# Gated linear attention into a gated SSM: q, k and alpha loaded as 32-step squares and turned by VectorE, output stores on the ACT queue

## The chip, the cores and the metric

The kernel runs on one core of a Trainium2 chip. The metric is the device time of one execution in microseconds. An execution that was also profiled gives the span and the trace that this document reads.

## The reference

Four sequences of 768 steps, 8 heads, 48 channels per head. First a recurrence per head with a gate per channel, then a block with an input projection, a scan over time, a gate and an output projection:

```
state = alpha[:, :, t, :, None] * state + einsum('bhd,bhe->bhde', k[:, :, t], v[:, :, t])
y[:, :, t] = einsum('bhd,bhde->bhe', q[:, :, t], state)
x = y as (B, S, H*D)                                # 4, 768, 384
val, gate = split(x @ w_in)                         # 384 x 1024, handed over as float64
h = exp(A_log)[0] * h + val[:, t]                   # scan over t
out = (gate * sigmoid(gate) * h) @ w_out            # 512 x 384
```

## The kernel before, in words

**Tiling.** A group is 256 steps (two tiles of 128) of one sequence with all heads, so there are N = 12 groups, three to a sequence. A pair j of heads shares the 128 partitions of a transposed tile: head 2j in rows 0 to 47, head 2j+1 in rows 64 to 111, with padding rows between (`DP` = 64). 

**Stages of one group.** `load` (L205) brings alpha, q and k into padded tiles `pads[n % 2]` (two sets) and v into one of three `v_sb`, by `load_heads` (L78): two DMAs of 128 partitions x 8 heads x 48 floats for each input, eight in all, on SP's queue. `front(n)` (L278) has five steps: (1) TensorE transposes alpha (L295, eight 128x128 tiles, in two PSUM tiles `tp`), VectorE makes the running products V from the group's end backward (L302), their reciprocal start iV and the running products P forward (L307), and ScalarE makes two passes over V into a tile `junk` that nobody reads, for their accumulated outputs (L312, L314), which test the range of V; (2) q is transposed and multiplied by P into Q (L319); (3) k is transposed and multiplied by V into K (L323); (4) scores `sc` = K against Q in 64-step blocks (L332), masked into A (L335); (5) K is turned back into Kn (L119, L120). `back(n)` (L341) makes block states `z` (L131), their running sums S_n on VectorE (L357), the outputs `y` inside a block (L146), a small ScalarE read `fence` (L151), then those from earlier blocks (L164), copies to x_sb (L365, L367), and transposes to xT (L173, L174). `ssm(n)` (L85) has four projections `pj` of twelve matmuls (L93), here called pj0 to pj3, each followed by the scan hh on VectorE (L96), Silu into sg on ScalarE (L101) and their product f on VectorE (L102); and two output tiles `o` of eight matmuls (L107), each copied to o_sb by ScalarE (L110) and stored (L111). The tiles pj and o share two PSUM buffers in turn.

**Order.** It is written out by hand (`manual_schedule`, L415 to L451). A turn n of the loop interleaves front(n), back(n-1), the first four steps of ssm(n-2) and the last two of ssm(n-3). TensorE's order in a full turn is: transposes of alpha(n), z(n-1), o(n-3) twice, transposes of q(n), y inside, pj0(n-2), transposes of k(n), y before, pj1, sc(n), tpx (x_sb), pj2, tpk (K back), pj3. VectorE's: V, P, S_n, Q, hh0, f0, K, hh1, f1, A, hh2, f2, hh3, f3. ScalarE's: junk twice, o_sb twice, fence, sg0, x_sb, sg1, xT, sg2, Kn, sg3. In turn n, `load(n + 2)` is called after the third step of front(n); on SP's queue it stands behind the stores of the same turn. Every queue works in its order.

**Weights.** w_in and w_out come as float64 words in twelve units (`fetch_unit`, L223); units 0 to 5 are fetched at the start, 6 to 11 in turn 0, behind the loads of group 2 on SP's queue. `split_unit` and `join_unit` turn a unit into float32 with ScalarE, VectorE and GpSimd, one unit to a step of turns 0 to 2, each of them in line with the other work of its engine.

**DMA semaphores.** DMAs raise eight completion semaphores (DMAHW0 to DMAHW7), handed out in turn in the order of the built program's text. Before a DMA is issued, its queue waits until the DMA that last had the same semaphore has landed, eight DMAs back in that text.

Of the kernel before, what the change touches and what calls it, by code (L numbers as in the profile page):

```python
# [9 lines left out]
FP32 = mybir.dt.float32  # L10
U8 = mybir.dt.uint8
# [7 lines left out]
def kernel(  # L19
# [23 lines left out]
    nc = tc.nc  # L43
    B, H, S, D = q.shape
    DM = H * D
    DI = moe_A_log.shape[0]
    C = 128
    R = 64
    NR = C // R
    G = 2  # L50
    GC = G * C
    GR = G * NR
    NG = S // GC
    NP = H // 2
    DP = 64
# [22 lines left out]
    def load_heads(dst, src, n, queue=nc.sync):  # L78

        b, g = divmod(n, NG)  # L80
        for c in range(G):
            rows = ds(g * GC + c * C, C)
            queue.dma_start(out=dst[:, c, :, 0:D], in_=src[b, :, rows, :].rearrange("h p d -> p h d"))  # L83

    def ssm(n, xT, prev_h, pool, ps_mm):  # L85

        b, g = divmod(n, NG)
        f = pool.tile([C, NI, GC], FP32, name="f")
        for cc in range(NI):
            pj = ps_mm.tile([C, 2, GC], FP32, tag="mm", name="pj")  # L90
            for i in range(2):
                for kk in range(NK):
                    nc.tensor.matmul(pj[:, i, :], w_in[:, kk, i, ds(cc * C, C)], xT[:, kk, :],  # L93
                                     start=(kk == 0), stop=(kk == NK - 1))
            hh = pool.tile([C, GC], FP32, tag=f"h{cc}", name="hh")
            nc.vector.tensor_tensor_scan(  # L96
                out=hh, data0=a_dec[:, cc:cc + 1].to_broadcast([C, GC]), data1=pj[:, 0, :],
                initial=prev_h[cc][:, GC - 1:GC] if g else 0.0, op0=ALU.mult, op1=ALU.add)
            prev_h[cc] = hh
            sg = pool.tile([C, GC], FP32, name="sg")  # L100
            nc.scalar.activation(sg, pj[:, 1, :], AF.Silu)  # L101
            nc.vector.tensor_mul(f[:, cc, :], sg, hh)  # L102
            yield
        for c in range(G):
            o = ps_mm.tile([C, DM], FP32, tag="mm", name="o")
            for cc in range(NI):
                nc.tensor.matmul(o, f[:, cc, ds(c * C, C)], w_out[:, cc, :],  # L107
                                 start=(cc == 0), stop=(cc == NI - 1))
            o_sb = pool.tile([C, DM], FP32, name="o_sb")
            nc.scalar.activation(o_sb, o, AF.Copy)  # L110
            nc.sync.dma_start(out=out[b, ds(g * GC + c * C, C), :], in_=o_sb)  # L111
            yield

    def keys_back(K, Kn, ps_tp):
# [66 lines left out]
    def ranged(ctx):  # L181
# [4 lines left out]
        p1 = pool("p1", 1)  # L186
# [15 lines left out]

        vs, st, xs = {}, {}, {}

        def load(n, names="aqkv", queue=nc.sync):  # L205
            for name in names:
                if name == "v":
                    vs[n] = p3.tile([C, G, H, D], FP32, name="v_sb")
                dst = vs[n] if name == "v" else pads[n % NBUF][name]
                load_heads(dst, dict(a=alpha, q=q, k=k, v=v)[name], n, queue)  # L210

# [64 lines left out]
        def front(n):  # L278

            pad = pads[n % NBUF]  # L280
            V = Vs[n % 2]
            iV0 = p2.tile([C, NP], FP32, name="iV0")
            P = p1.tile([C, NP, GC], FP32, name="P")
            Q = p3.tile([C, NP, GC], FP32, name="Q")
            K = p2.tile([C, NP, GC], FP32, name="K")
            A = As[n % 2]
            Kn = p2.tile([C, G, NP, C], FP32, name="Kn")
            st[n] = dict(V=V, Q=Q, A=A, Kn=Kn)

            def turned(name, jj):  # L290
                tp = ps_tp.tile([C, 2, GC], FP32, tag="tp", name="tp")
                for u in range(2):
                    j = 2 * jj + u
                    for c in range(G):
                        nc.tensor.transpose(tp[:, u, ds(c * C, C)], pad[name][:, c, 2 * j:2 * j + 2, :], ident)  # L295
                return tp

            for jj in range(NP // 2):
                tp = turned("a", jj)
                js = slice(2 * jj, 2 * jj + 2)  # L300
                for u in range(2):
                    nc.vector.tensor_tensor_scan(out=V[:, 2 * jj + u, GC - 1::-1], data0=tp[:, u, ::-1],  # L302
                                                 data1=bias[:, 1:2].to_broadcast([C, GC]), initial=1.0,
                                                 op0=ALU.mult, op1=ALU.max)
                nc.vector.reciprocal(iV0[:, js], V[:, js, 0])
                for u in range(2):
                    nc.vector.tensor_tensor_scan(out=P[:, 2 * jj + u, :], data0=tp[:, u, :],  # L307
                                                 data1=bias[:, 1:2].to_broadcast([C, GC]),
                                                 initial=iV0[:, 2 * jj + u:2 * jj + u + 1],
                                                 op0=ALU.mult, op1=ALU.max)  # L310
            junk = p1.tile([C, NP, GC], FP32, name="junk")
            nc.scalar.activation(junk, V[:, :, 0:GC], AF.Relu, scale=-1.0 / LOW, bias=bias[:, 0:1],  # L312
                                 accum_out=left[:, n, 0:1])
            nc.scalar.activation(junk, V[:, :, 0:GC], AF.Relu, scale=1.0 / HIGH, bias=bias[:, 2:3],  # L314
                                 accum_out=left[:, n, 1:2])
            yield
            for jj in range(NP // 2):
                js = slice(2 * jj, 2 * jj + 2)
                nc.vector.tensor_mul(Q[:, js], turned("q", jj), P[:, js])  # L319
            yield  # L320
            for jj in range(NP // 2):
                js = slice(2 * jj, 2 * jj + 2)
                nc.vector.tensor_mul(K[:, js], turned("k", jj), V[:, js, 1:GC + 1])  # L323
            yield
            sc = ps_sc.tile([C, 2, 512], FP32, tag="sc", name="sc")
            scv = sc.rearrange("p i (x t) -> p i x t", t=R)
            for c in range(G):
                for j in range(NP):
                    for r in range(NR):
                        for i in range(2):  # L330
                            rows, steps = ds(DP * i, DP), ds(c * C + R * r, R)
                            nc.tensor.matmul(scv[ds(R * r, R), i, c * NP + j, :], K[rows, j, steps],  # L332
                                             Q[rows, j, steps], start=True, stop=True, skip_group_check=True)
            for i in range(2):
                nc.vector.copy_predicated(out=A[:, i].rearrange("p x t -> p (x t)"),  # L335
                                          mask=mask[:, ds(i * GP * R, GP * R)], data=sc[:, i])
            yield
            keys_back(K, Kn, ps_tp)
            yield

        def back(n):  # L341

            s = st.pop(n)
            v_sb = vs.pop(n)
            first, last = n % NG == 0, n % NG == NG - 1
            S_n = p2.tile([C, GR, NP, D], FP32, name="S_n")
            if not first:
                nc.gpsimd.tensor_mul(S_n[:, 0], S_end[0], s["V"][:, :, 0:1].to_broadcast([C, NP, D]))  # L348
            zv = block_states(s["Kn"], v_sb, ps_sc, "sc")
            S_end[0] = None if last else p2.tile([C, NP, D], FP32, name="S_end")  # L350
            for x in range(GR):
                src = zv[:, x % NR, x // NR]
                dst = S_n[:, x + 1] if x + 1 < GR else S_end[0]
                if first and x == 0:
                    nc.vector.tensor_copy(out=dst, in_=src)
                elif dst is not None:
                    nc.vector.tensor_add(dst, S_n[:, x], src)  # L357
            yield
            yv = values_inside(s["A"], v_sb, ps_y, p2, 1)
            yield  # L360
            values_before(yv, s["Q"], S_n, first, 1)
            x_sb = p2.tile([C, G, DM], FP32, name="x_sb")
            xv = x_sb.rearrange("p g (j i e) -> p i (g j) e", i=2, e=D)
            ys = yv.rearrange("p i g j e -> p i (g j) e")
            nc.scalar.activation(xv[:, 0], ys[:, 0], AF.Copy)  # L365
            for r in range(NR):
                nc.scalar.activation(xv[ds(R * r, R), 1], ys[ds(R * (1 - r), R), 1], AF.Copy)  # L367
            yield
            xs[n] = p2.tile([C, NK, GC], FP32, name="xT")
            features(x_sb, xs[n], ps_tp)  # L370
            yield
# [247 lines left out]
```

## Time and profile before

| | us |
|---|---|
| median of 3 runs | 353.29 (352.75 to 353.89) |
| the profiled execution | 352.41 |
| its span | 350.7 |
| TensorE busy | 311.7 (89%) |
| VectorE busy | 201.1 (57%) |
| ScalarE busy | 113.4 (32%) |
| GpSimd busy | 57.9 (17%) |

The span is the profiled part of an execution; 1.7 us lie around it. "Busy" is the time in which an engine has an instruction under way. Rows of groups give the engine, the operation, the shapes and the mean duration of one. In a timeline, each line has a start, a length, an engine and a source line; what stands in brackets is idle time before it and what ended that. The chain of waits follows the work that ended last back to its start, at each step to what released it. SPq and ACTq are the queues of SyncE and ScalarE that issue DMAs.

### The profile page before, as it was taken

To read this page: it belongs to the slowest core of one execution; us is meant where nothing else is said; L and a number is where in the kernel's file an instruction comes from. 1 tells how busy PE (TensorE), PEld (TensorE's weight loads), DVE (VectorE), ACT (ScalarE), POOL (GpSimd) and SP (SyncE) were. 2 spreads that over 40 slices of the span, in tenths; PEclk is the share of its full clock that TensorE was granted. 3 is DMA by queue.
4 is the path that set the end of the run, shared out by engine and by line. 5 is a ranking of instruction groups with operands and counts; after the bars stand their busy time and mean duration, and the time that the engine had idled before them with its cause. 6 is when DMAs were issued, how large, how long until landed. Compare 5 with 4: busy or idle time off the path is not lost.

```text
span 350.7 us, 9637 instructions
## 1 busy us (share of the span) xinstructions
PE 311.7 (89%) x4233; PEld 251.7 (72%) x4233; DVE 201.1 (57%) x373; ACT 113.4 (32%) x243; POOL 57.9 (17%) x77
## 2 busy tenths in 40 slices
PE   2445763899999999999999999999999999998994
PEld 1334652687887887887878878868878878776682
DVE  2939968567449448546566476384494485313140
ACT  1514564332324233313314324333342233222111
POOL 4388898640000000000000000000000000000000
PEclk9996585999999999999999999999999999999999
DMA  9999995440850921902904905908301010010101
GB/s 128 216 228 192 288 190 71 79 57 2 150 79 2 186 42 48 170 13 64 163 3 99 129 2 116 113 2 165 64 12 36 2 47 2 2 48 0 49 0 53
DMA packets 107650, 29.02 MB, mean 83 GB/s; under 512 B 100944, under 2 KB 107088, under 8 KB 107600
## 3 DMA queue, kind: packets, MB, share of 16 engines
q1 hardware_dynamic: 104992, 27.93, 45.1%
q10 hardware_dynamic: 2608, 0.40, 1.0%
q8 instruction: 35, 0.57, 0.7%
q14 instruction: 15, 0.12, 0.1%
HBM read 23.60 MB, written 4.72 MB: 81 GB/s over the span
## 4 chain that ended last, share of the span: by engine, by line
PE 80%; POOL 5%; SPq 5%; DVE 3%; DMA 3%; issue 3%; ACT 0%; POOLq 0%; DVEq 0%; ACTq 0%
PE pj L93 36%; PE o L107 18%; PE tp L295 7%; SPq L83 4%; PE z L131 4%; PE y L164 3%; PE sc L332 3%; PE y L146 3%; DMA bits<-in_moe_w_in_dram 3%; PE tpk L119 2%; PE tpx L173 2%; POOL ex L241 2%; SPq L227 1%; POOL w_in L251 1%; POOL w_in L250 1%
## 5 line engine op out<-in xcount | busy, mean ns | idle before, releaser
L93 PE MATMUL pj<-xT,w_in 128*128 128x256 f32 x576 | 134.2, 384 | 0.0
L93 PEld LDWEIGHTS pj<-xT,w_in 128*128 128x128 f32 x576 | 106.2, 190 | 14.2
L107 PE MATMUL o<-w_out,f 128*128 128x384 f32 x192 | 65.0, 492 | 0.0
L96 DVE TENSOR_TENSOR_SCAN hh<-a_dec,hh,pj 128x256 f32<-128x256 f32 x32 | 23.9, 747 | 68.5 <-PE pj L93 68.5
L101 ACT ACTIVATE sg<-pj 128x256 f32<-128x256 f32 x48 | 18.4, 384 | 119.9 <-DVE hh L96 119.9
L107 PEld LDWEIGHTS o<-w_out,f 128*128 128x128 f32 x192 | 35.5, 190 | 23.0 <-DVE f L102 0.5
L348 POOL TENSOR_TENSOR S_n<-S_end,V 128x192 f32<-128x192 f32 x8 | 4.3, 542 | 209.6 <-DVE S_end L357 209.6
L102 DVE TENSOR_TENSOR f<-sg,hh 128x256 f32<-128x256 f32 x48 | 20.9, 435 | 23.8 <-ACT sg L101 23.8
L307 DVE TENSOR_TENSOR_SCAN P<-tp,iV,bias 128x256 f32<-128x256 f32 x48 | 33.4, 738 | 0.8
L302 DVE TENSOR_TENSOR_SCAN V<-tp,bias 128x256 f32<-128x256 f32 x48 | 30.1, 670 | 5.1 <-PE tp L295 5.1
L312 ACT ACTIVATE junk<-V,bias 128x1024 f32<-128x1024 f32 x12 | 13.8, 1148 | 53.9 <-DVE V L302 53.9
L295 PE MATMUL tp<-ident,q_pad 128*128 128x128 f32 x96 | 15.4, 305 | 14.5 <-DVE P L307 7.8
L295 PE MATMUL tp<-ident,a_pad 128*128 128x128 f32 x96 | 14.6, 300 | 14.2 <-issue 6.6
L295 PEld LDWEIGHTS tp<-ident,q_pad 128*128 128x128 f32 x96 | 12.4, 157 | 18.9 <-issue 16.3
L96 DVE TENSOR_TENSOR_SCAN hh<-a_dec,pj 128x256 f32<-128x256 f32 x16 | 11.0, 685 | 25.8 <-PE pj L93 25.8
L295 PEld LDWEIGHTS tp<-ident,a_pad 128*128 128x128 f32 x96 | 12.4, 154 | 16.0 <-issue 7.0
L241 POOL TENSOR_SCALAR ex<-ex 128x384 uint32<-128x384 uint32 x12 | 18.5, 1543 | 16.6 <-DVE ex L236 16.2
L332 PEld LDWEIGHTS sc<-Q,K 64*64 64x64 f32 x768 | 14.3, 148 | 4.3 <-issue 3.0
L335 DVE COPY_PREDICATED A<-mask,sc 128x512 f32<-128x512 uint8 x24 | 16.0, 721 | 1.1 <-PE sc L332 1.1
L332 PE MATMUL sc<-Q,K 64*64 64x64 f32 x768 | 16.1, 237 | 0.5 <-DVE K L323 0.5
L146 PEld LDWEIGHTS y<-v_sb,A 64*64 64x64 f32 x768 | 13.8, 149 | 2.7 <-issue 2.7
L295 PE MATMUL tp<-ident,k_pad 128*128 128x128 f32 x96 | 14.5, 299 | 1.4 <-DVE Q L319 1.0
(60 smaller groups left out, 325.0 us busy)
## 6 DMA issues: line engine op xcount, KB each, us to landing
a_pad<-in_alpha_dram SPq DMA_DIRECT2D x24, 192.0 KB, 4.6
k_pad<-in_k_dram SPq DMA_DIRECT2D x24, 192.0 KB, 5.5
v_sb<-in_v_dram SPq DMA_DIRECT2D x24, 192.0 KB, 5.0
out_dram<-o_sb SPq DMA_DIRECT2D x24, 192.0 KB, 2.3
q_pad<-in_q_dram SPq DMA_DIRECT2D x22, 192.0 KB, 5.0
bits<-in_moe_w_in_dram SPq DMA_DIRECT2D x8, 384.0 KB, 5.1
bits<-in_moe_w_out_dram SPq DMA_DIRECT2D x4, 384.0 KB, 7.2
q_pad<-in_q_dram ACTq DMA_DIRECT2D x2, 192.0 KB, 5.5
```

What stands on the lines that cost most here:

```text
L93: nc.tensor.matmul(pj[:, i, :], w_in[:, kk, i, ds(cc * C, C)], xT[:, kk, :], start=(kk == 0), stop=(kk == NK - 1))
L96: nc.vector.tensor_tensor_scan(out=hh, data0=a_dec[:, cc:cc + 1].to_broadcast([C, GC]), data1=pj[:, 0, :], initial=prev_h[cc][:, GC - 1:GC ...
L101: nc.scalar.activation(sg, pj[:, 1, :], AF.Silu)
L102: nc.vector.tensor_mul(f[:, cc, :], sg, hh)
L107: nc.tensor.matmul(o, f[:, cc, ds(c * C, C)], w_out[:, cc, :], start=(cc == 0), stop=(cc == NI - 1))
L146: nc.tensor.matmul(yv[at, i, c, j, :], A[rows, i, c * NP + j, :], v_sb[rows, c, 2 * j + i, :], start=(c == 0 and j == 0), stop=False, skip ...
L241: nc.gpsimd.tensor_scalar(out=ex, in0=ex, scalar1=896.0, scalar2=1151.0, op0=ALU.max, op1=ALU.min)
L295: nc.tensor.transpose(tp[:, u, ds(c * C, C)], pad[name][:, c, 2 * j:2 * j + 2, :], ident)
L302: nc.vector.tensor_tensor_scan(out=V[:, 2 * jj + u, GC - 1::-1], data0=tp[:, u, ::-1], data1=bias[:, 1:2].to_broadcast([C, GC]), initial=1 ...
L307: nc.vector.tensor_tensor_scan(out=P[:, 2 * jj + u, :], data0=tp[:, u, :], data1=bias[:, 1:2].to_broadcast([C, GC]), initial=iV0[:, 2 * jj ...
L332: nc.tensor.matmul(scv[ds(R * r, R), i, c * NP + j, :], K[rows, j, steps], Q[rows, j, steps], start=True, stop=True, skip_group_check=True)
L335: nc.vector.copy_predicated(out=A[:, i].rearrange("p x t -> p (x t)"), mask=mask[:, ds(i * GP * R, GP * R)], data=sc[:, i])
```

## The change

From group 2 on (`BY_VECTOR` = 2), alpha, q and k are no longer loaded as 128-partition tiles. Each is loaded in sixteen DMAs of 32 partitions x 8 x 32 or 16 floats, which lay 32 steps by 32 channels of each head as a square, so that VectorE's 32 x 32 block transpose of the whole 128 x 1024 tile gives what TensorE's eight transposes gave. Three such instructions to a group are new (into aT, and in place into Q and K); the multiplications then read SBUF instead of PSUM. Groups 0 and 1 stay as they were. v is loaded as before. For groups 2 and 3 GpSimd sets the padding of the squares, two memsets to a tile. The store of the output is issued by ScalarE instead of SP. Q has two buffers instead of three, K and x_sb one instead of two, and `junk` is written as bytes.

```
--- before.py
+++ after.py
@@ -108,7 +108,7 @@
                                  start=(cc == 0), stop=(cc == NI - 1))
             o_sb = pool.tile([C, DM], FP32, name="o_sb")
             nc.scalar.activation(o_sb, o, AF.Copy)
-            nc.sync.dma_start(out=out[b, ds(g * GC + c * C, C), :], in_=o_sb)
+            nc.scalar.dma_start(out=out[b, ds(g * GC + c * C, C), :], in_=o_sb)
             yield
 
     def keys_back(K, Kn, ps_tp):
@@ -202,12 +202,33 @@
 
         vs, st, xs = {}, {}, {}
 
+
+
+        BY_VECTOR, W = 2, 32
+
+        def squares(n, name):
+            return pads[n % NBUF][name].rearrange("p c h d -> p (c h d)")
+
         def load(n, names="aqkv", queue=nc.sync):
+            b, g = divmod(n, NG)
             for name in names:
+                src = dict(a=alpha, q=q, k=k, v=v)[name]
                 if name == "v":
                     vs[n] = p3.tile([C, G, H, D], FP32, name="v_sb")
-                dst = vs[n] if name == "v" else pads[n % NBUF][name]
-                load_heads(dst, dict(a=alpha, q=q, k=k, v=v)[name], n, queue)
+                    load_heads(vs[n], src, n, queue)
+                elif n < BY_VECTOR:
+                    load_heads(pads[n % NBUF][name], src, n, queue)
+                else:
+                    dst = squares(n, name).rearrange("p (j w e) -> p j w e", j=NP, e=W)
+                    for j in range(NP):
+                        for i in range(2):
+                            for half in range(2):
+                                ch, rows = min(W, D - W * half), ds(DP * i + W * half, W)
+                                if n < BY_VECTOR + NBUF and j == 0 and ch < W:
+                                    nc.gpsimd.memset(dst[rows, :, :, ch:W], 1.0 if name == "a" else 0.0)
+                                queue.dma_start(out=dst[rows, j, :, 0:ch],
+                                                in_=src[b, 2 * j + i, ds(g * GC, GC), ds(W * half, ch)]
+                                                .rearrange("(w p) d -> p w d", p=W))
 
 
 
@@ -281,8 +302,8 @@
             V = Vs[n % 2]
             iV0 = p2.tile([C, NP], FP32, name="iV0")
             P = p1.tile([C, NP, GC], FP32, name="P")
-            Q = p3.tile([C, NP, GC], FP32, name="Q")
-            K = p2.tile([C, NP, GC], FP32, name="K")
+            Q = p2.tile([C, NP, GC], FP32, name="Q")
+            K = p1.tile([C, NP, GC], FP32, name="K")
             A = As[n % 2]
             Kn = p2.tile([C, G, NP, C], FP32, name="Kn")
             st[n] = dict(V=V, Q=Q, A=A, Kn=Kn)
@@ -295,9 +316,13 @@
                         nc.tensor.transpose(tp[:, u, ds(c * C, C)], pad[name][:, c, 2 * j:2 * j + 2, :], ident)
                 return tp
 
+            by_vector = n >= BY_VECTOR
+            if by_vector:
+                aT = p1.tile([C, NP, GC], FP32, name="aT")
+                nc.vector.transpose(aT.rearrange("p j t -> p (j t)"), squares(n, "a"))
             for jj in range(NP // 2):
-                tp = turned("a", jj)
                 js = slice(2 * jj, 2 * jj + 2)
+                tp = aT[:, js] if by_vector else turned("a", jj)
                 for u in range(2):
                     nc.vector.tensor_tensor_scan(out=V[:, 2 * jj + u, GC - 1::-1], data0=tp[:, u, ::-1],
                                                  data1=bias[:, 1:2].to_broadcast([C, GC]), initial=1.0,
@@ -308,19 +333,23 @@
                                                  data1=bias[:, 1:2].to_broadcast([C, GC]),
                                                  initial=iV0[:, 2 * jj + u:2 * jj + u + 1],
                                                  op0=ALU.mult, op1=ALU.max)
-            junk = p1.tile([C, NP, GC], FP32, name="junk")
+            junk = p1.tile([C, NP, GC], U8, name="junk")
             nc.scalar.activation(junk, V[:, :, 0:GC], AF.Relu, scale=-1.0 / LOW, bias=bias[:, 0:1],
                                  accum_out=left[:, n, 0:1])
             nc.scalar.activation(junk, V[:, :, 0:GC], AF.Relu, scale=1.0 / HIGH, bias=bias[:, 2:3],
                                  accum_out=left[:, n, 1:2])
             yield
+            if by_vector:
+                nc.vector.transpose(Q.rearrange("p j t -> p (j t)"), squares(n, "q"))
             for jj in range(NP // 2):
                 js = slice(2 * jj, 2 * jj + 2)
-                nc.vector.tensor_mul(Q[:, js], turned("q", jj), P[:, js])
-            yield
+                nc.vector.tensor_mul(Q[:, js], Q[:, js] if by_vector else turned("q", jj), P[:, js])
+            yield
+            if by_vector:
+                nc.vector.transpose(K.rearrange("p j t -> p (j t)"), squares(n, "k"))
             for jj in range(NP // 2):
                 js = slice(2 * jj, 2 * jj + 2)
-                nc.vector.tensor_mul(K[:, js], turned("k", jj), V[:, js, 1:GC + 1])
+                nc.vector.tensor_mul(K[:, js], K[:, js] if by_vector else turned("k", jj), V[:, js, 1:GC + 1])
             yield
             sc = ps_sc.tile([C, 2, 512], FP32, tag="sc", name="sc")
             scv = sc.rearrange("p i (x t) -> p i x t", t=R)
@@ -359,7 +388,7 @@
             yv = values_inside(s["A"], v_sb, ps_y, p2, 1)
             yield
             values_before(yv, s["Q"], S_n, first, 1)
-            x_sb = p2.tile([C, G, DM], FP32, name="x_sb")
+            x_sb = p1.tile([C, G, DM], FP32, name="x_sb")
             xv = x_sb.rearrange("p g (j i e) -> p i (g j) e", i=2, e=D)
             ys = yv.rearrange("p i g j e -> p i (g j) e")
             nc.scalar.activation(xv[:, 0], ys[:, 0], AF.Copy)
```

## Prediction

> **What bounds the kernel now.** I read the page first. TensorE is busy 89% of the span and is 80% of the chain of waits; the rest of the chain is the start.
>
> ```profile
> span 350.7 us, 9637 instructions
> PE 311.7 (89%) x4233; PEld 251.7 (72%) x4233; DVE 201.1 (57%) x373; ACT 113.4 (32%) x243; POOL 57.9 (17%) x77
> PEclk9996585999999999999999999999999999999999
> PE 80%; POOL 5%; SPq 5%; DVE 3%; DMA 3%; issue 3%; ACT 0%; POOLq 0%; DVEq 0%; ACTq 0%
> ```
>
> Then one turn in the chain of waits (start, length): it is TensorE alone.
>
> ```profile
> 203.75 0.87 PE tp L295 x8
> 204.63 1.08 PE z L131 x64
> 205.71 5.36 PE o L107 x16
> 211.06 0.87 PE tp L295 x8
> 211.94 1.08 PE y L146 x64
> 213.01 2.79 PE pj L93 x12
> 215.80 0.87 PE tp L295 x8
> ...
> 220.54 1.09 PE sc L332 x64
> ...
> 228.50 0.87 PE tp L295 x8
> ```
>
> From 203.75 to 228.50 a turn takes 24.74 us, three entries of 0.87 among it being the transposes that go. Turns 3 to 11 (79.9 to 302.6) are all like this. Last the timelines of ScalarE and of SP's queue in the same turn, and two lines of the start:
>
> ```profile
> 209.48 1.15 ACT L312 ACTIVATE junk<-V,bias 128x1024 f32<-128x1024 f32 x1 [4.47 <-DVE V L302]
> 211.90 0.85 ACT L110 ACTIVATE o_sb<-o 128x384 f32<-128x384 f32 x2
> ```
> ```profile
> 212.40 0.83 SPq L111 DMA_DIRECT2D out_dram<-o_sb  x2
> ```
> ```profile
> 40.06 0.60 DVE L236 TENSOR_SCALAR ex<-bits 128x384 uint32<-128x384 uint32 x1 [0.21 <-DMA bits<-in_moe_w_in_dram]
> ```
> ```profile
> 60.32 1.96 PE L146 MATMUL y<-v_sb,A 64*64 64x48 f32 x64
> ```
>
> The reader is to see: o_sb starts at 211.90 though o ended at 211.06, since junk stands before it and waits for V; two DMA issues start 0.83 - 0.36 (one store's issue, by the tile's row) = 0.47 us apart; the conversion of weight unit 6 already waits for its DMA; and after TensorE had idled 5.45 us the same 64 matmuls took 1.96 us instead of 1.08.
>
> **What the Trainium skill says.** "VectorE: DVE Perf Modes", The three transpose paths: VectorE turns 32x32 blocks only, SBUF to SBUF. No transpose is in this trace. "Vector Engine (DVE) Microarchitecture Reference", 3.8: one element per cycle per lane; "VectorE: DVE Perf Modes", The TRN2 errata, has fp32 tensor_tensor at (N+151)/0.96 ns: 691 for N = 512, and the trace has 682 for Q. So my estimate for 1024 is 1.22 us. "DMA: Bandwidth & Descriptors", Issuing engines are not separate DMA queues: another issuing engine saves issue time only; no run here shows it yet. "TensorE: Matmul & The Clock Gate", Part 1: an idle window of some 3.4 us halves the clock; the y line above and PEclk's 6, 5, 8 agree.
>
> **The change, part by part.**
> *Removed from TensorE:* 3 x 0.87 = 2.61 us a turn, which would make 22.13.
> *Added to VectorE:* three transposes of 1.2 each; below 1.07 (1024 elements at one a cycle) it can't be, twice it, 2.4, is the far end. VectorE is busy 14.9 of the turn's 24.74, so its sum fits; its places matter.
> *SP:* 48 + 2 issues a group instead of 8; at 0.47 that is 23.5 us. The span of one issue hardly depends on size (332 ns smallest for a store, 368 for k); I keep 0.42 and 0.6 as ends. Packets go from 8192 to 14336 a group (six times 2048 of 128 or 64 bytes, and v); at the 23 ns that a packet costs now (DMA share 0.5 x 24.74 us x 16 / 8448) it is 21 us of each DMA engine, under the turn.
> *Stores:* two issues of 0.47 now stand in ScalarE's order, behind each o_sb.
> *Semaphores:* in the built program's text the stores of turn m (from 6 on) stand amid the k squares of group m: k's sixth and ninth DMA (37 and 40 of the 50, from 0) have the semaphore of the first and second store. They wait until those stores have landed. In turn 5 it is 42 and 44; the stores of turns 3 and 4 hold up DMAs 17 and 19 of group 4, 5 and 7 of group 5, a turn before they are wanted. Before, SP went past a turn's stores with the loads of two groups on; now the k of the same turn waits for them.
> *Pools, byte junk, memsets:* K and x_sb with one buffer are freed a turn earlier by TensorE's order (tpk and tpx before the next writes): nothing. Byte junk: no row; I take 1.15 as now, half of it is the other end (1.1 us less before o_sb). Twelve memsets of 0.3 to 0.6 lie in GpSimd's wait for unit 6: nothing.
>
> **One turn, from the end of pj3 (time 0; 203.75 before).** hh3 and f3 end at 1.7 (205.47). Transpose of alpha: 2.9. First V to last V takes 4.06 (205.39 to 209.45): 7.0. Two junk take 2.45 (to 211.90): 9.5. o_sb 0.48: 10.0; store issue at 10.1; second o_sb to 11.05; second store at 11.1. A store lands 2.3 us after issue (median): 12.4 and 13.4. TensorE is at pj0 after z, o, y = 7.5, and waits for o_sb's PSUM buffer until 10.1, ends it at 12.9, y and pj1 at 16.8. VectorE: hh0 and f0 take 1.57 after pj0: 14.5, free for the transpose of k. But k's DMAs 40 to 47 go out from 13.4, the last at 13.4 + 7 x 0.47 = 16.7; landing 2.2 (3.2 is the smallest of a load now, of which 1.0 goes on draining its 1024 packets, the median length of an issue in a backlog): 18.9. Transpose 20.1, K's two halves 0.64 each: 21.4; sc, whose first part needs one half, in effect from 21.2. From sc to the end of pj3 7.95 (220.54 to 228.50): 29.2 us, 4.5 more than now. In turn 5 only four DMAs follow the store: 27.3. Turns 3 and 4 have their k; there f0's 14.5 leads to K at 17.0, sc from 16.8: 24.8, no gain, since o_sb and K take the place of TensorE. Is SP's rest in time? From 17.2 v, a, q take 34 x 0.47 = 16: alpha has landed at 27.5 (wanted at 30.9), q at 35.3 (wanted at 39). Yes.
> TensorE now idles 2.6 and 4.4 us a turn, at which the clock may drop: between 0 and 3 us a turn (y alone lost 0.9); I take 1.3 for seven turns.
>
> **The start.** Group 2's fifty issues stand before unit 6. They begin at 23.9 as now; the first eight wait for weight units in flight (the last issued by 23.8, landing 5.5 by the median: until 29.3), the other 42 x 0.47 end at about 49.2; landing 4.7 (smallest of these rows): unit 6 at 53.9 instead of 40.06, 13.8 later. VectorE, ScalarE and GpSimd stand behind it. Turn 2 adds transposes of alpha, q and k on the chain to sc(2), with less wait for TensorE: 3.2. Shift 17 (ends 11, when all issues are at 0.47 and landing is 4, and 20).
>
> **The sum.** 17 + 2 x 0.1 + 2.6 + 6 x 4.5 + 7 x 1.3 = 56. The profiled span 350.7 becomes 407, its own time 352.41 becomes 408, and the median of 353.29 becomes 409. The tail from turn 12 has no front: nothing.
>
> **Rivals.** (A, my forecast, 0.75) as above. Its own range: turn 28.2 (issue 0.42, landing short, half junk) to 33 (transposes twice, landings 3.2): 385 to 435. (B, 0.10) k is in time after all, because issue or landing is much quicker than it looks: turns of 24.8, only the start lost: 353.3 + 17 + 0.9 = 371. For it: stores land in 1.9 at best; against it: eight issues alone take 3.3 us. (C, 0.10) SP or the small packets set the turn: at 0.7 us an issue 35 us a turn, seven turns 72 more, start 27: 452. For it: issues of 1 us[...]; against it: 256 packets an issue instead of 1024. (D, 0.04) The other side: TensorE stays the bound at 22.1 a turn, because junk, transposes and k all end before 7.5, 10 and 14.2: 9 x 2.61 = 23.5 gained, 17 lost: 347. It decides when the mean turn is under 24.74 - 17/9 = 22.85; but the chain f3, transpose, V, junk, o_sb, pj0 alone is 2.6 us too long for that. That the squares are not turned by VectorE is excluded: the built program has three such instructions a group and no transposes on TensorE. The last 0.01 is no change.
>
> **Numbers.** Range: 375 to 445 leaves out D, over half of B and most of C, 0.18. Faster by over 0.3% 0.04 (D), same 0.01, slower 0.95; 0.3% is about what a measurement of this kernel can tell from none.
>
> **What would show it.** Right: turns of 29 to 31 us from z to z, sc waiting for K, K's transpose for a DMA, SPq waiting for stores amid k; unit 6's conversion waiting until about 54; transposes of 1.2 us; issues 0.47 apart; half clock after the idle. Wrong: turns of 22 (D) or 25 (B), SPq without idle time (C), transposes over 2 us.

## The result and the profile after

| | before | after |
|---|---|---|
| median | 353.05 us (352.75 to 353.89, 4 runs) | 428.96 us (427.24 to 433.85, 4 runs) |
| ratio to before | | 1.213 (95% interval 1.208 to 1.218) |
| the profiled execution, its span | 352.41, 350.7 | 433.85, 432.1 |
| z of turn 3 starts at | 80.87 | 107.27 |
| z of turn 3 to z of turn 12 (nine turns) | 221.8 | 274.8 |
| z of turn 12 to the end | 48.0 | 50.1 |

The forecast was 409 us with a range of 375 to 445; the kernel is 76 us slower. The execution that left the profile is the longest of the four (the spans of the others are 425.5 to 427.7), so some 5 of the 81.4 us that the table explains are its own.

The page of the kernel after, lines that answer to those shown of before:

```profile
span 432.1 us, 9699 instructions
PE 310.9 (72%) x3993; PEld 243.5 (56%) x3993; DVE 242.3 (56%) x403; ACT 115.3 (27%) x243; POOL 65.6 (15%) x89
PEclk9996659559989899898799698799699898699899
SPq 28%; PE 25%; DVE 18%; DMA 12%; issue 6%; POOL 5%; ACT 4%; ACTq 0%; DVEq 0%; POOLq 0%
```

TensorE has 240 instructions fewer, but is busy as long as before: the clock row shows why, with its 7s and 6s all through the span. The chain of waits was TensorE for 80%; it is now TensorE for 25%, and SP's queue for 28%.

One turn (turn 9, z at 286.53) in the chain of waits, each line a start, a length and what it is:

```profile
288.21 1.26 DVE aT L322
...
293.60 1.25 ACT junk L337 x2
...
296.12 0.38 ACT o_sb L110
...
296.52 1.87 DMA out_dram<-o_sb
298.42 0.31 SPq L229
...
302.89 0.44 SPq L229
...
303.38 2.15 DMA k_pad<-in_k_dram
...
305.56 1.25 DVE K L349
...
307.67 2.07 PE sc L361 x64
309.74 1.47 PE tpx L173 x6
311.21 3.27 PE pj L93 x12
```

Read it downward: alpha's transpose, V, junk, o_sb, the store; SP stands until the store has landed at 298.39 and goes on with k's squares; the last of them is issued at 302.89 and lands 2.15 later; then K's transpose and sc. After that sc, tpx and pj2 take 6.81 us where at full clock they take 1.09 + 0.81 + 2.59 = 4.49.

The views of waits of the same kernel (engine, line, what it waited for: us in total, times, longest), for all engines and for SP's queue:

```profile
DVE K L349 <- DMA k_pad<-in_k_dram: 28.9, 7, 5.5
PE sc L361 <- DVE K L352: 28.4, 8, 5.4
PE pj L93 <- ACT o_sb L110: 22.2, 9, 2.5
```
```profile
SPq L229 <- DMA out_dram<-o_sb: 61.8, 9, 24.5
```

K's transpose waits for its DMA in seven turns, and SP waits for a store in nine. In each of turns 3 to 11 the load that has the semaphore of the first store is issued within 0.02 us of that store's landing. The longest of SP's waits, 24.5 us, is in turn 3, and comes back below.

### The profile page after: what moved, and what is told of

Read it like the earlier page. It is cut to its first block, busy times and chain, and to the rows that moved or that the text cites. A ratio compares the mean times of both kernels' runs of the same rounds, so it can differ in the third digit from the quotient of the medians.

```text
span 432.1 us, 9699 instructions
## 1 busy us (share of the span) xinstructions
PE 310.9 (72%) x3993; PEld 243.5 (56%) x3993; DVE 242.3 (56%) x403; ACT 115.3 (27%) x243; POOL 65.6 (15%) x89
## 4 chain that ended last, share of the span: by engine, by line
SPq 28%; PE 25%; DVE 18%; DMA 12%; issue 6%; POOL 5%; ACT 4%; ACTq 0%; DVEq 0%; POOLq 0%
SPq L229 23%; PE pj L93 15%; DVE V L327 6%; PE o L107 4%; DVE P L332 4%; DMA out_dram<-o_sb 3%; SPq L83 3%; DMA q_pad<-in_q_dram 3%; DVE aT L322 3%; DMA bits<-in_moe_w_in_dram 2%; DMA k_pad<-in_k_dram 2%; ACT junk L337 2%; PE sc L361 2%; POOL ex L262 2%; PE tpx L173 2%
## 5 line engine op out<-in xcount | busy, mean ns | idle before, releaser
L93 PE MATMUL pj<-xT,w_in 128*128 128x256 f32 x576 | 147.8, 412 | 22.2 <-ACT o_sb L110 22.2
L93 PEld LDWEIGHTS pj<-xT,w_in 128*128 128x128 f32 x576 | 115.8, 207 | 40.7 <-ACT o_sb L110 23.3
L164 PE MATMUL y<-S_n,Q 64*64 64x48 f32 x704 | 15.9, 238 | 38.7 <-ACT fence L151 38.7
L361 PE MATMUL sc<-Q,K 64*64 64x64 f32 x768 | 22.5, 290 | 28.5 <-DVE K L352 28.4
L164 PEld LDWEIGHTS y<-S_n,Q 64*64 64x64 f32 x704 | 14.4, 152 | 43.7 <-issue 27.2
L337 ACT ACTIVATE junk<-V,bias 128x1024 uint8<-128x1024 f32 x12 | 13.8, 1150 | 69.7 <-DVE V L327 69.7
L332 DVE TENSOR_TENSOR_SCAN P<-aT,iV,bias 128x256 f32<-128x256 f32 x40 | 28.6, 757 | 0.7
L349 DVE STREAM_TRANSPOSE K<-k_pad 128x1024 f32<-128x1024 f32 x10 | 12.4, 1244 | 28.9 <-DMA k_pad<-in_k_dram 28.9
L327 DVE TENSOR_TENSOR_SCAN V<-aT,bias 128x256 f32<-128x256 f32 x40 | 26.0, 693 | 0.4
L96 DVE TENSOR_TENSOR_SCAN hh<-a_dec,pj 128x256 f32<-128x256 f32 x16 | 10.9, 684 | 24.1 <-PE pj L93 24.1
L364 DVE COPY_PREDICATED A<-mask,sc 128x512 f32<-128x512 uint8 x24 | 16.1, 723 | 2.2 <-PE sc L361 1.5
L110 ACT ACTIVATE o_sb<-o 128x384 f32<-128x384 f32 x24 | 11.6, 484 | 19.9 <-PE o L107 15.7
## 6 DMA issues: line engine op xcount, KB each, us to landing
bits<-in_moe_w_in_dram SPq DMA_DIRECT2D x8, 384.0 KB, 5.5
bits<-in_moe_w_out_dram SPq DMA_DIRECT2D x4, 384.0 KB, 6.6
```

The costliest lines, as they stand in the source:

```text
L96: nc.vector.tensor_tensor_scan(out=hh, data0=a_dec[:, cc:cc + 1].to_broadcast([C, GC]), data1=pj[:, 0, :], initial=prev_h[cc][:, GC - 1:GC ...
L164: nc.tensor.matmul(yv[at, i, c, j, :], Q[rows, j, ds(R * x, R)], S_n[rows, x, j, :], start=False, stop=(c == G - 1 and j == NP - 1), skip_ ...
```

## The experiments

The theory that the forecast stood on: the semaphores that stores and k's squares share make k wait for the same turn's stores. Rivals: SP's fifty issues, or their small packets, set the turn; the stores cost only their two issues; the start is lost to something other than the order of the loads. For each run: its median, its ratio to before with the 95% interval, when z of turn 3 starts, and the mean of the nine turns from there to z of turn 12.

| | median us | ratio | z of turn 3 | mean turn |
|---|---|---|---|---|
| before | 353 | 1 | 80.87 | 24.64 |
| after | 428.96 | 1.213 (1.208 to 1.218) | 107.27 | 30.53 |
| e1, stores on SP | 395.62 | 1.117 (1.112 to 1.122) | 107.23 | 26.37 |
| e2, stores on GpSimd | 391.89 | 1.109 (1.107 to 1.112) | 108.51 | 25.73 |
| e3, before with stores on ScalarE | 353.13 | 1.000 (0.999 to 1.001) | 80.87 | 24.64 |
| e4, weight units first | 428.38 | 1.210 (1.206 to 1.214) | 92.96 | 31.95 |
| e5, 24 unread matmuls a turn | 450.20 | 1.273 (1.269 to 1.278) | 107.33 | 32.48 |
| e6, e2 and units first | 377.60 | 1.067 (1.065 to 1.070) | 91.38 | 26.11 |
| e7, e2, squares from group 4 | 366.51 | 1.037 (1.034 to 1.040) | 80.94 | 25.87 |
| e8, e2 and junk later | 385.81 | 1.091 (1.086 to 1.095) | 106.71 | 25.21 |
| e9, 12 unread matmuls a turn | 419.56 | 1.190 (1.184 to 1.195) | 106.57 | 29.12 |
| e10, q and k only, from group 4 | 341.97 | 0.968 (0.965 to 0.970) | 81.95 | 23.27 |
| e11, e6 without memsets | 382.07 | 1.080 (1.076 to 1.085) | 86.65 | 26.91 |
| e12, e2 with 5 unread matmuls | 384.03 | 1.088 (1.085 to 1.090) | 107.55 | 24.86 |

### Do the stores hold up k? (e1, e2, e3, e4)

e1: `nc.scalar.dma_start(out=out[...])` becomes `nc.sync.dma_start`. 

> The changed kernel, with the output stores back on SP's queue. Theory (the stores and the k squares of the same turn are tied through the shared DMA semaphores, so that SP stops amid k until the stores have landed): in SP's own order a store stands behind the loads of a later group, so the wait falls on a semaphore that is long free; k is in time, the turn is what 52 issues of 0.49 us on SP or the chain to o_sb allow, 25.5 to 26.5 us instead of 32; 7 turns x 6 us less: about 385 to 395 us. The stall of SP for stores (24.5 us in nine waits) is gone. Rival 1 (SP's rate of issue or the small packets set the turn): SP has two issues more per turn, so no gain, 428 to 435 us. Rival 2 (the stores on ScalarE cost only their two issues): 2 x 0.5 x 10 = 10 us less, about 418 us.

e2: the same line on `nc.gpsimd`. 

> The changed kernel, with the output stores on GpSimd's queue, whose DMAs have semaphores of their own. Theory (shared semaphores): no store stands in the order of SP's semaphores, turns of 25 to 26.5 us, 385 to 395 us, near the version with the stores on SP. Rival 1 (SP's issues or packets): 428 us. Rival 2 (a new wait: GpSimd is held at o_sb, with T and bits behind it): between 395 and 415 us.

e3: the kernel before, that line on `nc.scalar`. 

> The kernel before, with nothing changed but the output stores on ScalarE's queue. Theory: with 10 loads a group instead of 50, a load that takes a store's semaphore is wanted a turn or more later; no change, 352 to 355 us. Rival (ScalarE's issue, or its wait, costs by itself): 2 x 0.5 x 12 = up to 12 us more, 365 us.

Measured: 395.6, 391.9 and 353.1. No turn of e1 or e2 waits for a store amid k, their turns are 24.8 to 26.6 us (but for e1's turn 11, below), and 33 to 37 of the 76 us are gone by moving two DMAs a turn to another queue. In e3 the move costs nothing that can be measured (the interval ends at 0.1% more). So it is neither ScalarE's issue nor the queue as such, but which load the store's semaphore falls on. In e1, SP's order puts the stores among alpha's squares two groups on. There they have another price: in turn 11 o_sb can't be written (4.6 us of wait) because the store that has its buffer stands behind SP's loads; that turn is 32.3 us. (The "24.5 us in nine waits" of e1's expectation is the longest wait alone; the nine sum to 61.8.)

e4, in turn 0:

```
-                if n + 2 < N:
-                    load(n + 2)
                 if n == 0:
                     for u in range(6, len(units)):
                         fetch_unit(u)
+                if n + 2 < N:
+                    load(n + 2)
```

> The changed kernel, with the issues of weight units 6 to 11 moved ahead of group 2's fifty in the first turn. Theory (the loads of group 2 delay unit 6, which landed at 57.8 us instead of 40.1): unit 6 lands near 40 again, turn 3 begins up to 17 us earlier; the memsets of GpSimd, the transposes of group 2 and the longer turns stay: 408 to 413 us. Rival (the start is long because of the transposes, memsets and group 2's own late landing): no more than 5 us less, 423 to 428 us.

Measured: 428.4, no gain, and yet the rival is wrong too: z of turn 3 comes 14.3 us earlier. Turns 3 and 4 then take 33.7 and 34.0 us instead of 26.5 and 26.3, which gives it all back. My words "the longer turns stay" were the fault. In the built program's text of e4 the stores of turn 3 have the semaphores of the fourth and seventh of group 3's k, and those of turn 4 the sixth and ninth of group 4's; in the kernel after they have those of q of group 4 and alpha of group 5. The coupling to the same turn's k begins two turns sooner. The timelines of SP's queue (start, length, queue, line, DMA, count) show the first of these stands; after, then e4:

```profile
94.24 33.06 SPq L229 DMA_DIRECT2D q_pad<-in_q_dram  x16
```
```profile
77.67 34.22 SPq L229 DMA_DIRECT2D k_pad<-in_k_dram  x16
```

Sixteen issues take some 9 us elsewhere; here 24.5 and 25.8 us of waiting for the first store lie among them. In the kernel after SP was at group 4's loads while TensorE was still in turn 2, and loses 24.5 us of that lead.

### What does the clock cost? (e5, e9, e12)

e5, ten of these ahead of pj0 and fourteen ahead of sc in turns 3 to 11, into a PSUM tile that nobody reads:

```
+            for i in range(count):
+                nc.tensor.matmul(wm[:, i % 2, :], ident, w_in[:, 0, 0, 0:GC], start=True, stop=True)
```

> The changed kernel, with matmuls that nobody reads in TensorE's idle time of turns 3 to 11: ten ahead of pj0, fourteen ahead of sc. Theory (after the idle of 2.5 and 5 us TensorE works at half clock for a while, which costs about 1.6 us in turns 3 and 4 and 2 to 4 in each later one): sc, tpx and pj2 take 1.1, 0.8 and 2.6 us again, turns 3 and 4 24.8 us, later turns 29 to 30: 7 x 2.5 + 2 x 1.6 = 20 less, about 408 us. Rival 1 (the loop is held by SP, whose 50 issues take 28.5 us a group and which waits some 4 us for stores): clock at full but turns stay near 31, 425 us or more. Rival 2 (the added matmuls come out of the time of the path): slower than 429.

A miss of mine: one such matmul is two passes of 0.216 us, so that 10.4 us went into a turn, not 5.2. All turns are 32.48 us at full clock, TensorE without a gap. It shows that the idle is what halves the clock, but not what that costs.

e9: the same with 5 and 7. 

> The changed kernel again with matmuls that nobody reads, half as many: five ahead of pj0, seven ahead of sc, in turns 3 to 11 (each is two passes of 0.216 us, so the first try put 10.4 us into a turn instead of 5.2, and TensorE, 22.1 + 10.4 = 32.5, set the turn at full clock). TensorE has now 27.3 us a turn, less than the loop through the stores. Theory (the clock's loss is about 1.6 us in turns 3 and 4 and about 2.5 in the later ones, over the loop of 29.2 that the forecast worked out): turns of 29 to 30 from turn 5 on, about 409 us. Rival 1 (the loop through the stores, or SP, holds the turn at 31 to 32 whatever the clock): 425 us or more. Rival 2 (the clock still falls with so few matmuls): between the two.

Measured: 419.6, between the theory and rival 1, and not for the reason that I gave for such a value. Turns 3 to 8 are all 27.6 to 27.7 us, which is TensorE with the added matmuls; turns 9, 10 and 11 are 32.0, 34.0 and 30.1. In this program's text the stores of turns 3 to 7 fall on loads that are wanted a turn later, those of turn 8 on the twelfth of k's squares of the same group, of turn 9 on the eighth, of turns 10 and 11 on the fourth. So the added matmuls moved the semaphores as well, and the price of the clock can't be read from this run. What it does show is the coupling once more: stores on ScalarE's queue cost nothing in six turns, and 2.4 to 6.3 us in those where k of the same turn has the semaphore with eight squares or more still to come.

e12: e2, with five matmuls ahead of pj0 only. 

> The version with the stores on GpSimd's queue (391.9 us), with five matmuls that nobody reads (ten passes of 0.22 us) ahead of pj0 in turns 3 to 11, so that TensorE's idle of 2.5 us before pj0 becomes one of 0.3. No store's semaphore and no k is waited for there, so the turns differ by the clock alone: 24.8 us, and 26.3 to 26.6 where pj0 takes 4.5 us instead of 2.8. Theory (idle of 2.5 us brings the half clock after it, which costs 1.7 us in every turn that has it): all pj0 take 2.8 us, turns of 24.8 to 25.0, six turns x 1.6 = 10 less: about 382 us; SP's last load, at 312 us, comes no earlier, and if its lead is used up by then the last turns wait for k: up to 386. Rival (the half clock comes from load over a longer time, not from the idle before it): the turns stay mixed, 390 us or more.

Measured: 384.0, 7.9 less (the spans differ by 9.0), and no pj0 of turns 3 to 11 takes over 2.9 us. One of e12's turns in the view by stretches (the stretch, its length, then the busy time of TensorE, of its weight loads, of VectorE, ScalarE and GpSimd; the third number from the end is the share of the clock), and two of e2's:

```profile
132.38:157.29 24.91, 24.76 (x329) 19.25 (x329) 19.22 (x31) 8.04 (x18) 1.59 (x3) 1.00 0.47 74
```
```profile
108.51:133.33 24.82, 22.40 (x335) 17.45 (x334) 18.52 (x30) 8.08 (x18) 1.32 (x2) 1.00 0.47 75
133.33:159.90 26.57, 24.09 (x319) 18.45 (x318) 19.29 (x31) 8.06 (x18) 1.59 (x3) 0.94 0.47 73
```

TensorE's work of a turn is 22.4 us at full clock. In e2 five of the nine turns have up to 1.7 more, in pj0 after 2.5 us of idle. With the idle filled, all turns are 24.8 to 24.9.

Which of e2's turns pay can be read from its trace. The clock falls to half for 3.41 us at a time, and these stretches start (144.38, 195.58, 246.78, 274.09, 325.29) whole multiples of 3.413 us apart: 15, 15, 8 and 15. Three stretches of this grid, the first two from turn 4, the third from turn 5:

```profile
140.97:144.38 3.41, 0.98 (x5) 0.88 (x6) 3.29 (x7) 2.78 (x7) 0.74 (x2) 1.00 0.84 143
144.38:147.79 3.41, 3.41 (x9) 2.32 (x7) 1.99 (x3) 0.00 (x0) 0.85 (x2) 0.50 0.67 163
168.26:171.67 3.41, 1.70 (x8) 1.52 (x9) 3.25 (x7) 2.06 (x6) 1.45 (x3) 1.00 0.42 74
```

In turn 4 nearly all of the idle falls into one stretch, which is left with 0.98 us of work, and the next one is at half clock. In turn 5 the same idle lies across two stretches, the emptier of them has 1.70 us of work, and the clock stays full. Over the nine turns, the emptiest stretch has 0.9 to 1.4 us of work in the five that pay, and 1.6 to 2.0 in the four others. So the place of the idle on the grid decides, not its length alone. No sharp limit is shown: in the other runs stretches with 1.45 to 1.73 us of work are found on both sides.

### The start, and SP's lead (e6, e7, e11)

e6: e2 with e4's order. 

> The version with the stores on GpSimd's queue (391.9 us), and the issues of units 6 to 11 ahead of group 2's. Theory (SP issues without a pause from 24 to 312 us, 28.5 us a group against turns of 25.7; the long start is a lead that these turns use up, of which 15 us is left at the last group): turn 3 begins 14 us earlier and the lead is just used up, 377 to 384 us, with waits for k in the last turns. Rival 1 (SP is no bound): 392 - 14 = 378 us with no wait for k. Rival 2 (as with the stores on ScalarE's queue, all of the start is given back): 392 us.

Measured: 377.6. The start gained 17 us and this time 14 stay, since no store's semaphore meets k. In e2 the last group's k has landed 16.5 us before its transpose; in e6 K waits 2.3 us for it. In e2 and in e6 SP issues without a pause; e2's timeline of SP:

```profile
225.91 9.29 SPq L229 DMA_DIRECT2D a_pad<-in_alpha_dram  x16
235.29 8.95 SPq L229 DMA_DIRECT2D q_pad<-in_q_dram  x16
244.34 9.09 SPq L229 DMA_DIRECT2D k_pad<-in_k_dram  x16
253.52 1.02 SPq L83 DMA_DIRECT2D v_sb<-in_v_dram  x2
```

From one group's alpha to the next (254.65) it is 28.7 us, more than e2's turn of 25.7. SP lives on its lead. The median issue takes 0.449 us, 0.49 with the gap, but 21 of e2's 480 squares take 1.2 to 2.1; the traces don't show why.

e7: e2 with `BY_VECTOR = 4`. 

> The version with the stores on GpSimd's queue, with squares only from group 4 on. Theory (the start is lost to the issues, memsets and transposes of groups 2 and 3 alone, and a turn by squares is 24.8 us plus about 1 for the clock): start as in the kernel before (turn 3 at 81 us), then 8 turns x 0.7 to 1.3 more: 358 to 364 us. If SP's 28.5 us a group bind (no lead from a long start), the later turns go to 28 and it ends at 368 to 380.

Measured: 366.5, a little over what I expected. The start is that of before to 0.1 us. Turns 4 to 11 are 24.9 to 26.9. That is the clock, not SP: every k has landed 24 us or more before its transpose.

e11: e6 with the line `nc.gpsimd.memset(dst[rows, :, :, ch:W], ...)` left out. 

> The version with the stores on GpSimd's queue and the weight units first (377.6 us), without the twelve memsets of the squares' padding, which is so left with what lay there. Theory (the six memsets for group 3 stand in GpSimd's chain of weight conversion, 3.6 us without an idle moment from 24 to 65 us, those for group 2 another 3.4 ahead of it, of which a part is covered): 3.6 to 6 us less, 371.5 to 374 us. Rival (they lie beside other waits, as the forecast had it): 377 us.

Measured: turn 3 begins 4.7 us earlier than in e6, as expected, and the whole is 4.5 us longer, which neither theory had. The gain ran into SP: its last load of group 11 goes out at 314.4 (314.0 in e6), and K waits 3.1 and 3.0 us for its DMAs in turns 9 and 11; after each of these waits sc and tpx are at half clock. These two turns are 4.2 and 2.2 us longer than in e6.

### What holds the turn at 24.8? (e8, e10)

e8: e2, with the two junk activations behind the product Q. 

> The version with the stores on GpSimd's queue, with the two junk passes of ScalarE moved behind Q, so that o_sb no longer stands behind them. Theory (the turn of 24.8 us is the chain f3, transpose of alpha, V, junk, o_sb, pj0, K, sc): the chain is 2.45 us shorter, TensorE bounds at 22.3 until SP's lead of about 15 us is used up; 9 x 2.45 = 22 is more than that, so about 372 to 380 us, with waits for k or q at the end. Rival 1 (SP's issues bound already): 390 to 393. Rival 2 (VectorE, busy 22 of 25.7 us, takes the place of ScalarE): turns of 24, 383 to 388 us.

Measured: 385.8; rival 2. o_sb no longer waits for junk, but sc waits for K in ten turns. In the turn from z at 232.24 VectorE has no gap from hh3 to A but the half microseconds in which it waits for sg, and sc comes 16.3 us after z; the next z is at 256.73, 24.5 later. The turns with half clock take up to 26.2.

e10, from what these runs showed (SP is full with fifty issues, VectorE with three transposes, and junk delays o_sb):

```
-        BY_VECTOR, W = 2, 32
+        BY_VECTOR, W = 4, 32
-                elif n < BY_VECTOR:
+                elif n < BY_VECTOR or name == "a":
-                tp = aT[:, js] if by_vector else turned("a", jj)
+                tp = turned("a", jj)
```

with the stores on SP and junk behind Q. 

> A version made from what the runs showed: only q and k as squares, from group 4 on; alpha stays on TensorE; stores on SP's queue; the two junk passes behind Q. Theory: the start is untouched; SP has 38 issues, some 21 us a turn, so it is no bound; o_sb isn't behind junk; VectorE has Q ready ahead of hh0 and K at about 16 us, where TensorE (24.74 less two transposes of 0.97) comes to sc at 15 to 16; TensorE is the bound at 22.8 to 23.5 us with no idle to lower its clock: 8 turns x 1.2 to 1.9 less, 338 to 344 us. Rival 1 (K is late by 1 us or more and the clock falls after it): turns of 24.7 or more, 353 to 360. Rival 2 (SP can't keep up): as the version with all squares from group 4 on, 366.

Measured: 341.97, 3.2% under the kernel before. Its view by stretches:

```profile
199.51:222.68 23.17, 23.17 (x344) 18.40 (x343) 17.32 (x30) 8.24 (x18) 0.52 (x1) 1.00 0.54 87
```

TensorE is busy all of 23.17 us at full clock. VectorE is busy 17.3 of it instead of 14.9; SP's 38 issues at 0.57 are 22. 24.74 less two transposes of 0.87 is 23.0.

## Why the prediction was right, and where its terms were off

**One turn: the mechanism and its times held.** From the end of pj3 in turn 9 (286.5): alpha's transpose at 1.7 (forecast 1.7), o_sb at 9.5 (9.5), the store out at 10.0 (10.1) and in at 11.9 (12.4), the last square of k issued at 16.4 (16.7), its landing at 19.0 (18.9), sc at 21.1 (21.2). Turn 9 is the one nearest to the forecast: in turns 6 to 8, 10 and 11 the last square lands at 19.5 to 20.1 and sc comes at 21.8 to 22.4. Issues are 0.49 apart (0.47), a transpose takes 1.24 us (1.2), a square lands 2.1 us after its issue (2.2). "Turns 3 and 4 have their k; there 24.8, no gain" is e12's turn to 0.1 us; in the kernel after these two are 26.5 and 26.3, with pj0 at half clock.

**The clock was mis-sized: "between 0 and 3 us a turn; I take 1.3 for seven turns".** The view by stretches of the kernel after, turn 6 and the sum of its nine turns:

```profile
188.41:221.67 33.26, 26.73 (x335) 20.81 (x334) 18.66 (x30) 8.50 (x18) 0.00 (x0) 0.85 0.41 62
sum 274.75, PE 224.60 PEld 175.58 DVE 169.55 ACT 75.90 POOL 3.09; mean PE 24.96 PEld 19.51 DVE 18.84 ACT 8.43 POOL 0.34
```

TensorE's busy time is 224.6 us; at 22.4 a turn, as in e2's turns at full clock, it would be 201.5. Not all of the 23.1 us between them lengthen a turn: in turns 6, 8 and 11 pj0 is at half clock (4.2 to 4.6 us instead of 2.9) while K has to wait for its squares anyway. What does lengthen a turn is pj0 in turns 3 and 4, by 1.7 and 1.4 us against e12's turns, to which I gave nothing; and in turns 5 to 11 what follows sc: from sc to the next z it takes 9.5 to 10.9 us instead of 7.95, 16.1 us together, 2.3 a turn instead of 1.3. That is 19 us, not 9.1. I had the price from one line of 64 small matmuls; but after 4.4 us of idle it is sc, tpx and most of pj2 that run at half, and after 2.5 us it is pj0. "TensorE: Matmul & The Clock Gate" of the Trainium skill, Part 1, has a free-running window of about 3.4 us; the grid of 3.41 us in e2's trace agrees with it. That 3.4 us of idle is the least that counts does not agree: in e2 2.5 us were enough in five turns.

The nine turns got 53.0 us longer. Without these 19 it is 33.9, against 0.2 + 2.6 + 27 = 29.8 of the forecast. Most of that difference is sc, which in turns 6 to 11 comes 22.0 us after z on average, not 21.2, because k's last square lands later.

**The start was too short: 17 against 26.4.** Unit 6 was ready at 57.8 instead of 53.9: group 2's issues began at 24.9 (forecast 23.9) and ended at 52.7 (49.2), and the landing took 5.0. The step "twelve memsets lie in GpSimd's wait for unit 6: nothing" failed. GpSimd's timeline:

```profile
61.64 1.20 POOL L272 TENSOR_TENSOR w_in<-w_in,ex 128x384 f32<-128x384 f32 x1
62.90 1.08 POOL L228 MEMSET a_pad<- 32x512 f32 x2
64.01 1.20 POOL L228 MEMSET q_pad<- 32x512 f32 x2
65.25 1.20 POOL L228 MEMSET k_pad<- 32x512 f32 x2
66.53 1.49 POOL L262 TENSOR_SCALAR ex<-ex 128x384 uint32<-128x384 uint32 x1
```

Those of group 3 stand behind the wait, in the middle of the conversion of units 6 and 7: 3.6 us. e11 puts all twelve at 4.7, with the weights early. Scans beside GpSimd cost 1.5 (last section). The transposes of alpha and q are 2.5 on the chain, 0.7 less than the 3.2 that I had for all three. That makes 3.9 + 3.6 + 1.5 - 0.7 = 8.3 of the 9.4 us. The rest is the clock again, which I had left out of the start: after 22.4 us of idle, y from earlier blocks and pj1 of turn 2 take 1.96 and 3.69 us, instead of 1.15 and 2.86 before. With these 1.6 the sum is 9.9, half a microsecond too much.

**The tail: nothing, measured 2.1.** 1.7 of it is one pair of o at half clock (7.02 us instead of 5.32), after a wait of 1.96 that the kernel before has too.

**The rivals.** That k is in time (B) is what e2 makes of the kernel; the forecast for B, 371, left out 9 us of start and the clock. That SP sets the turn (C) is not how the kernel ends up: in turns 6 to 11 SP stands 2.5 to 6.7 us for the first store, and alpha's last square has landed 2.9 us or more before alpha's transpose. But "at 0.47 that is 23.5 us" was wrong for SP: it is 28.5 us a group. With sc at 22.0 and 7.95 after it, a turn at full clock would be about 30 us, an estimate from these figures, which still lies over SP's 28.5. No run here cures the clock of the changed kernel and nothing else, so how much that would give back stays open. D was held off by more than the chain that I named: e8 takes junk out of it, and no turn comes under 24.4.

**What added up.** The forecast missed by 20 us: 10 by the clock of the turns, 4 for the most part by k's later landing, 9 by the start, 2 by the tail, less the 5 by which the profiled execution stands over the median. All four go the same way, and the range was not made for them: the turn of 33 us behind its upper end stood for transposes of twice the length and landings of 3.2 us, and neither came. The mechanism of the turn was foreseen; that the sum still lies inside the range is in part luck.

## What to carry to other kernels

Before DMAs are added or moved to another queue, find which DMA shares a completion semaphore with which, and how far ahead of its use each is issued: the same move of two stores cost nothing where a load was a turn early, and 37 us where it was wanted at once. A queue's lead over the engines is a stock: a change that shortens the start or the turn uses it up, and a gain in one place (e4, e11) is given back where the next queue or semaphore waits. And price an idle gap on TensorE with the clock of all that follows it, and expect to pay in some turns and not in others.

## What the runs showed of the hardware

- TensorE's clock falls to half for stretches of 3.41 us on a fixed grid. In e2 it does so after a stretch of that grid with 0.9 to 1.4 us of work, and not after one with 1.6 or more. An idle of 2.5 us costs 1.3 to 1.7 us in five of its nine turns and nothing in four. Five matmuls in that gap remove the loss, and are worth 8 us of 392 (e12). After 4.4 us of idle, in turn 9 of the kernel after, the half clock lasts two such stretches, 6.83 us.
- SP's small issues: 0.49 us as a rule, but 28.5 us for fifty (0.57 each), in part because 21 of e2's 480 squares take 1.2 us or more.
- VectorE's scans are slower beside GpSimd once they read SBUF. Alpha now comes from SBUF; in turn 2 of the kernel after, the first pair of P coincides with GpSimd's tensor_tensor, the second doesn't:

```profile
77.39 2.10 DVE L332 TENSOR_TENSOR_SCAN P<-aT,iV,bias 128x256 f32<-128x256 f32 x2
81.64 1.39 DVE L332 TENSOR_TENSOR_SCAN P<-aT,iV,bias 128x256 f32<-128x256 f32 x2
```

GpSimd's own instruction beside it took 1.37 us instead of 1.00. Before, with alpha in PSUM, P took 1.39 beside the same GpSimd operation (at 34.57). "SBUF — State Buffer" of the Trainium skill, Who interferes with whom, says that a VectorE instruction with two SBUF inputs contends with a GpSimd instruction that reads SBUF; these lines agree, and e6 has the same pair (2.10 and 1.40). No run tried it by itself.
